# The first product of an MLP by seven products: the operands of the next block made by a table of 42 places

## The chip, the cores and the metric

The kernel runs on one core of one Trainium2 chip. The core has five engines with a queue of instructions each, taken strictly in order: TensorE (PE, with its weight loads as PEld), VectorE (DVE), ScalarE (ACT), GpSimd (POOL) and SyncE (SP), which here issues nearly all DMAs. An instruction that waits holds up everything behind it on its own engine. The metric is device time in microseconds (us) of one execution, lower is better.

## The reference

Two layers of self-attention and MLP run on a row matrix x of 2048 x 640 in float32, with a layer norm without weights ahead of each part:

```
x = x + attention(layernorm(x))         # 32 heads of 20
x = x + mlp(layernorm(x))               # 640 -> 1536 -> 640
mlp(y) = relu(y @ w1 + b1)**2 @ w2 + b2
(both lines twice, with the same weights)
```

What is changed here lies around `layernorm(x)` and `y @ w1`.

## The kernel before

Every layer has these stages: attention; the **heads** stage, which multiplies the attention's output by `wo` and adds x (`add_heads`); the **up** stage, the first product of the MLP (class `Up`); and the **down** stage, the second (class `Down`).

**Heads.** The 2048 rows are handled as 16 tiles of 128 rows, four tiles to a block, four blocks. A tile takes two chains of 15 matmuls, one per half of the 640 columns, each into a PSUM bank of its own; the banks are used in a ring of eight. After a chain DVE adds the old x (L1407), then a call of `side()` takes one step of side work, and after two chains SP stores the new row tile to `d_x`.

**Up.** Each block of 512 rows is multiplied by w1 with Strassen's scheme in Winograd's form: seven products of half-size matrices in place of eight. On the side of w1 the seven operands (A11, S2, S1, A22, S3, A12, S4) are made once and stored; on the side of the rows the operands are B11, T2, T1, T4, T3, B21, B22 for the first 512 of the 640 columns, and a plain part and a difference (`xd`) for the last 128. They are sums of four row tiles of the block: tiles 0 and 1 make one half, 2 and 3 the other, and the sums are formed of the pairs (0, 2) and (1, 3). Every float32 operand is split in two parts, a rounded one (`hi`, a copy by ACT, L375) and the rest (`lo`, a subtraction by DVE, L376, or by POOL, L342, for T3 and T4). A product is three matmuls per 128 columns: hi by hi, hi by lo, lo by hi.

A **unit** of the up stage is one of six column groups of w1: chains of 6 (A11), 9 (S4, of the unit before), 6 (S2), 6 (S1), 9 (A22), 9 (S3) and 9 (A12) matmuls, 54 in all, into four banks; the next unit uses the other four. S3 adds into the bank of S2, A12 into that of A11 and S4 into that of S1. DVE's own work in a unit, in its order: L1488 (after the S4 chain), L1465 (after S2; the S3 chain waits for it), then L1473, L1474 and L1475 after S3 (the next S4 chain waits for L1474). ACT does copies, bias with relu, and squares (L1454, L1460, L1477, L1490), POOL two sums at the unit's end (L1493, L342), SP the store of the result (`d_h`).

Between the chains of a unit `side()` is called seven times, 42 times in a block; each call runs one step that makes the operands of the **next** block. A **place** is the number of such a call in its block: place 7k + s is call s of unit k. Calls 2, 3 and 4 lie, for DVE, between L1465 and L1473; calls 5 and 6, and 0 of the next unit, between L1475 and L1488; call 1 between L1488 and L1465.

To make the operands of a block, each of its four row tiles is loaded (`x<-d_x`), its mean and variance taken (`stats`: L315 and L316 on DVE, L318 and L319 on POOL), normalised and turned in blocks of 32 (`turn`: L348 and L353 on DVE), stored to `d_t`, and read back across partitions by four DMAs (`turn_load`: `y<-d_t`). Then come the sums on POOL (L342) and the splits on ACT, DVE and POOL.

Before, all that is one generator, `forms`, whose `yield`s set the places. It takes about 31 of the 42 places of a block, from place 0 on: loads at place 0, `stats` of two tiles at 3 and 4, the first sums and the first split one line after the other in one place, and the split of T2 in the next. For block 0 the generator is run in the last two of the four blocks of the heads stage, three steps per call, and what is left is run at once at the end.

The arena of 42 slots holds the pieces of w1 (24 slots), the operands of two blocks and the results; SP allows eight DMAs to be under way.

Of the kernel before, what the change touches and what calls it, by code (L numbers as in the profile page):

```python
# [16 lines left out]
P = 128  # L17
# [5 lines left out]
KD = D // P  # L23
# [18 lines left out]
def tile_layers(  # L42
# [320 lines left out]
    def forms(qb, x_src, res, late):  # L363

        xs, ys, mvs = {}, {}, {}

        def view(y):
            return y.rearrange("p (a k i) -> p k a i", a=4, k=KD)

        def split(dst, src, i, lo):  # L370
# [4 lines left out]
            nc.scalar.copy(hi_, src)  # L375
            lo(lo_, src, hi_.bitcast(F32))  # L376

        def pair(i):
            a, b = view(ys[i]), view(ys.pop(i + 2))
            t = xtile("t").rearrange("p (k a i) -> p k a i", a=4, k=KD)  # L380
            k1, k2, k3 = slice(0, 2), slice(2, 4), slice(4, 5)
            if not res:
                for n in range(LAST + 2):
                    if n == LAST + 1:
                        res[n] = xpool.tile([P, 2, 1, 2 * P], F32R, tag="x", name=name("xd"))
                    elif n != B21 or not late:
                        res[n] = slot([P, 2, 2, 2 * P], F32R, "xf")
            dve = nc.vector.tensor_sub
# [7 lines left out]
            split(res[T1_], t[:, k1], i, dve)  # L396
            yield
            pool_lo(t[:, k3], a[:, k3], b[:, k3])
            pool_lo(t[:, k2], a[:, k2], t[:, k2])
            split(res[B22], b[:, k2], i, dve)  # L400
            yield
            split(res[T4_], t[:, k2], i, pool_lo)
            yield
            split(res[T3_], b[:, k1], i, pool_lo)
            yield
            for r, y in enumerate((a, b)):
                split(res[LAST][:, :, r : r + 1], y[:, k3], i, dve)
            split(res[LAST + 1], t[:, k3], i, dve)
            yield
            if not late:  # L410
                split(res[B21], a[:, k2], i, dve)
                del ys[i]
                yield

        def rest():
            res[B21] = slot([P, 2, 2, 2 * P], F32R, "xf")
            for i in range(2):
                split(res[B21], view(ys.pop(i))[:, 2:4], i, nc.vector.tensor_sub)

        def load(i):  # L420
            xs[i] = row_tile(x_src, qb * 4 + i)

        def turned(i):
            ys[i] = turn(xs[i], mvs.pop(i), i)
            del xs[i]

        load(0)
        load(2)
        yield
        yield  # L430
        yield
        for i in (0, 2):
            mvs[i] = stats(xs[i])
            yield
        load(1)
        load(3)
        yield
        for i in (0, 2):
            turned(i)
            yield  # L440
            yield
        for i in (1, 3):
            mvs[i] = stats(xs[i])
            yield
        turn_load(ys[0], 0)
        turned(1)
        yield
        turn_load(ys[2], 2)
        yield
        turned(3)  # L450
        yield
        yield
        yield
        turn_load(ys[1], 1)
        for n, _ in enumerate(pair(0)):
            if n == 1:
                turn_load(ys[3], 3)
            yield
        yield from pair(1)
        if late:  # L460
            late.append(rest)
# [1239 lines left out]
    def layer(first, x_a, x_m, x_e, front_0, ahead):  # L1701
# [26 lines left out]
        coming = first_forms = None  # L1728
# [10 lines left out]
        for _ in first_forms:  # L1739
            pass  # L1740
# [11 lines left out]
        firsts = list(range(16, w_1.n))  # L1752
        up = Up(side)
        for qb in range(NQB):
            nxt, late = {}, []
            if qb + 1 < NQB:
                late.append(None)
                coming_rows = forms(qb + 1, x_m, nxt, late)
                for n in range(7 * NP - 1):
                    steps.append(lambda n=n, f=coming_rows: (  # L1760
                        n % 2 == 1 and firsts and w_1.load(firsts.pop(0)), next(f, None)
                    ))
# [104 lines left out]
```

## Time and profile before

| what | before |
|---|---|
| median of 3 runs | 3612.69 us (3606.93 to 3617.94) |
| the profiled execution, and its span | 3612.81 us, 3610.7 us |
| busy PE, DVE, ACT, POOL | 97%, 77%, 79%, 27% of the span |
| matmuls of the up stage (L1427), idle ahead of them | 74.4 us |
| heads stage of the two layers, about | 1373 to 1444 us, 3172 to 3243 us |
| up stage of the two layers, about | 1444 to 1651 us, 3243 to 3453 us |
| mean granted clock of PE | 0.988 |

The profile is one execution on the chip. Matmuls are pipelined and overlap, so the busy share of PE says little of how much it does; idle time just before a group of instructions, and what ended it, says more. In rows of a timeline the columns are the start, the length, engine, line, operation, names and shapes, a count where rows were merged, and in square brackets the idle time of that engine just before and the instruction that ended it. Rows "SPq" are DMAs being issued.

### The profile page before, as it was taken

The numbers are of one execution on the slowest core, as the hardware profiler recorded it, in microseconds if no ns is written. First come the engines' busy times: TensorE is split into PE (matmuls) and PEld (weight loads), VectorE is DVE, ScalarE is ACT, GpSimd is POOL, SyncE is SP. The second block draws the span as 40 slices with busy tenths as digits, with TensorE's granted clock in tenths as the row PEclk, the third lists the DMA queues.
The fourth block names the chain that finished last, engine by engine and source line by source line (L and its number), as shares of the span: only waits on it lengthen the run. The fifth ranks groups of instructions, "written<-read, shape, count | busy, mean of one in ns | idle before, by whom it ended". The sixth has DMA issues, their size and how long they took to land. (4 is left out here: it accounts for less than half of the span.)

```text
span 3610.7 us, 74267 instructions
## 1 busy us (share of the span) xinstructions
PE 3519.4 (97%) x26404; PEld 2177.0 (60%) x26404; DVE 2771.0 (77%) x5512; ACT 2834.9 (79%) x5026; POOL 965.2 (27%) x1189
## 2 busy tenths in 40 slices
PE   9999999999999999789999999999999999997999
PEld 8997333333333338789989973333333333387899
DVE  8998888888888863556869988888888888545567
ACT  5889999999999992354348899999999999913533
POOL 4430444444412211340153202211221122113400
PEclk9999999999999999899999999999999999998999
DMA  7665444444322147648667652222232211476484
GB/s 258 223 217 179 133 146 145 123 136 126 119 61 57 48 125 258 233 159 299 230 195 231 194 165 66 69 81 60 63 83 56 56 50 51 131 267 221 170 288 147
DMA packets 335041, 534.46 MB, mean 148 GB/s; under 512 B 75604, under 2 KB 154964, under 8 KB 334672
## 3 DMA queue, kind: packets, MB, share of 16 engines
q1 hardware_dynamic: 334144, 528.02, 45.9%
q8 instruction: 209, 3.42, 0.4%
q10 hardware_dynamic: 528, 1.70, 0.2%
q14 instruction: 160, 1.31, 0.1%
HBM read 339.01 MB, written 190.55 MB: 147 GB/s over the span
## 5 line engine op out<-in xcount | busy, mean ns | idle before, releaser
L905 ACT ACTIVATE e<-banks 128x512 f32<-128x512 f32 (+1 forms) x3416 | 2035.2, 691 | 56.7 <-PE banks L895 20.3
L812 DVE TENSOR_REDUCE mx<-banks 128x1 f32<-128x512 f32 x2560 | 1620.5, 685 | 321.9 <-PE banks L801 269.2
L910 PE MATMUL banks<-e,vg 128*32 128x512 f32 x8192 | 1093.5, 605 | 2.1 <-ACT e L905 2.0
L801 PE MATMUL banks<-k,q 60*128 60x512 f32 x3360 | 1060.3, 410 | 0.0
L895 PE MATMUL banks<-q,k 62*128 62x512 f32 x4096 | 1049.7, 441 | 1.6 <-DMA d_v<-v 0.3
L895 PEld LDWEIGHTS banks<-q,k 62*128 62x128 f32 x4096 | 514.9, 184 | 749.5 <-ACT e L905 441.3
L801 PEld LDWEIGHTS banks<-k,q 60*128 60x128 f32 x3360 | 567.8, 185 | 195.1 <-ACT e L905 63.9
L841 DVE CUSTOM_DVE_ANT_0 rl<-banks,rl 128x512 f32<-128x512 f32 x736 | 477.0, 689 | 31.3 <-PE banks L801 7.0
L834 ACT ACTIVATE rl<-banks 128x512 f32<-128x512 f32 x736 | 399.6, 602 | 57.4 <-PE banks L801 45.7
L1427 PE MATMUL banks<-xf,w 128*128 128x256 f32 x2448 | 331.6, 297 | 74.4 <-DVE r L1474 64.9
L910 PEld LDWEIGHTS banks<-e,vg 128*32 128x32 f32 x8192 | 162.2, 108 | 352.9 <-issue 269.9
L1427 PEld LDWEIGHTS banks<-xf,w 128*128 128x128 f32 x2448 | 320.7, 205 | 81.9 <-DVE r L1474 68.6
L508 PE MATMUL banks<-xnT,wqk 64*128 64x512 f32 x1080 | 326.6, 392 | 0.0
L496 PE MATMUL banks<-xnT,wqk 64*128 64x512 f32 x1080 | 325.6, 393 | 0.0
L954 POOL TENSOR_TENSOR few<-few,minus_t 128x16 f32<-128x16 f32 x62 | 179.9, 2902 | 236.1 <-DMA few<-d_s 236.0
L339 POOL CAST mr<-nt 128x32 fp32r<-128x32 f32 x64 | 13.6, 212 | 751.1 <-DVE nt L867 751.1
L965 POOL TENSOR_TENSOR o<-o 128x512 f32<-128x512 f32 x62 | 79.6, 1284 | 500.1 <-DMA o<-d_r 276.6
L801 PE MATMUL banks<-kd,q 60*128 60x512 f32 x736 | 210.8, 398 | 1.1 <-ACT rl L834 0.5
L496 PEld LDWEIGHTS banks<-xnT,wqk 64*128 64x128 f32 x1080 | 199.2, 186 | 11.5 <-issue 1.7
L508 PEld LDWEIGHTS banks<-xnT,wqk 64*128 64x128 f32 x1080 | 201.2, 187 | 7.0
L496 PE MATMUL banks<-wv,xnT 64*128 64x320 f32 x960 | 193.5, 308 | 0.0
L1454 ACT ACTIVATE r<-r,b_t 128x512 f32<-128x512 f32 x96 | 59.2, 616 | 170.9 <-DVE r L1475 149.2
(149 smaller groups left out, 3656.4 us busy)
## 6 DMA issues: line engine op xcount, KB each, us to landing
q<-d_qk SPq DMA_DIRECT2D x876, 80.0 KB
d_qk<-ev SPq DMA_DIRECT2D x80, 512.0 KB
k<-d_qk SPq DMA_DIRECT2D x444, 80.0 KB
x<-d_x SPq DMA_DIRECT2D x96, 320.0 KB
w<-d_w SPq DMA_DIRECT2D x60, 480.0 KB
w<-d_w SPq DMA_DIRECT2D x48, 512.0 KB
d_h<-r SPq DMA_DIRECT2D x48, 512.0 KB
r<-d_h SPq DMA_DIRECT2D x48, 512.0 KB
```

The lines of the kernel that those rows point to most:

```text
L496: top = nc.tensor.matmul(dst, a[:64], b[:64], start=start, stop=last)
L508: low = nc.tensor.matmul(dst, a, b, start=False, stop=last, skip_group_check=True)
L801: nc.tensor.matmul(dst, q_t[t][b : b + 60, p, sub * P : (sub + 1) * P], k_t[t // NQB, c][b : b + 60, p, :], start=True, stop=True,)
L812: nc.vector.tensor_reduce(maxima(t)[:, 2 * p + par, sub, c : c + 1], dst, axis=AX.X, op=ALU.max)
L834: nc.scalar.activation(r, dst, AF.Relu)
L841: nc.vector.tensor_tensor_reduce(out=r[par], in0=dst, in1=r[par], scale=1.0, scalar=LEAST, op0=ALU.add, op1=ALU.max, accum_out=maxima(t)[: ...
L895: nc.tensor.matmul(dst, k_t[t // NQB, kt // 4][b : b + 62, p, (kt % 4) * P : (kt % 4 + 1) * P], q_t[t][b : b + 62, p, :], start=True, stop ...
L905: nc.scalar.activation(dst, src, AF.Exp, scale=SCALE)
L910: nc.tensor.matmul(acc[32 * h : 32 * h + 32, :], v_t[t // NQB, kt // 8][:, kt % 8, 32 * h : 32 * h + 32], es[p][:, par, :], start=(kt == 0 ...
L954: nc.gpsimd.tensor_tensor(few, few, minus_t, op=ALU.pow)
L965: nc.gpsimd.tensor_mul(o[:, 0, :], o[:, 0, :], o[:, 1, :])
L1427: nc.tensor.matmul(dst, w, v, start=n == 0 and not more, stop=n == len(todo) - 1, skip_group_check=more,)
```

## The change

The generator becomes a class `Forms` with one method for each step, and two tables say at which place which step stands. `PLACES` holds for the making of a block during the up stage of the block before: it uses the 42 places of that block and, by numbers below zero, the last nine places of the block before that (-9 is place 33, -4 place 38, -3 place 39). `BESIDE_HEADS` holds for block 0, by the number of the call in the heads stage (0 to 31); the steps -9, -4 and -3 of block 1 stand at calls 29, 30 and 31 there.

Loads, `stats`, `turned`, `fetch` (the four `y<-d_t` DMAs), sums and splits are now separate entries. The T1 and T2 splits stand three and four places behind their sums for the pair (0, 2) and three and five for (1, 3); T4's and T3's order is changed. The slots of the operands are taken when each is first written.

Also moved: the 24 pieces of w1 (`w_1.load`, 512 KB each) are loaded one at a time, 18 of them at calls 2 to 22 of the heads stage, two at 25 and 27, and the last four at places 1, 4, 7 and 10 of block 0 (before: four after each heads block, 16, and eight at odd places of block 0). In the last block the first reads of the down stage (`lead`) stand at places 27, 29 and 33 instead of 35, 36 and 39, and the rows at 31 instead of 37. No arithmetic is changed: each engine has as many instructions as before. The lines are shifted: L1407 is now L1441, L1465 L1499, L1473 to L1475 L1507 to L1509, L1488 L1522, L375 and L376 L458 and L459.

The core of the diff:

```diff
-    def forms(qb, x_src, res, late):
...
-            pool_lo(t[:, k1], b[:, k1], a[:, k1])
-            pool_lo(t[:, k2], b[:, k2], t[:, k1])
-            split(res[B11], a[:, k1], i, dve)
-            yield
-            pool_lo(b[:, k1], b[:, k2], b[:, k1])
-            split(res[T2_], t[:, k2], i, dve)
-            yield
...
+    class Forms:
+        PLACES = {
+            -9: [("load", 0), ("load", 2)],
+            -4: [("stats", 0)],
...
+            23: [("sums", 0), ("split", B11, 0)],
...
+            27: [("split", T2_, 0)],
...
+        BESIDE_HEADS = {
+            10: [("load", 0), ("load", 2)],
+            12: [("stats", 0)],
...
+        def do(self, places, n):
+            for what, *args in places.get(n, ()):
+                getattr(self, what)(*args)
...
-        for qb in range(NQB):
-            if qb == 2:
-                first_forms = forms(0, x_m, x := {}, [])
-            if qb > 1:
-                steps.extend([lambda: [next(first_forms, None) for _ in range(3)]] * 7)
-            add_heads(qb, x_a, x_m, xs, side)
-            for s in range(qb * 4, qb * 4 + 4):
-                w_1.load(s)
...
+        weights_at = {g: 1 for g in [*range(2, 8), *range(9, 15), *range(17, 23), 25, 27]}
...
+        def between():
+            side()
+            n = beside[0]
+            made[0].do(Forms.BESIDE_HEADS, n)
+            made[1].do(Forms.PLACES, {29: -9, 30: -4, 31: -3}.get(n))
+            more(weights_at.get(n, 0))
+            beside[0] += 1
...
-                todo = {35: down.fetch, 37: lambda: down.rows(0), 36: down.fetch, 38: down.make,
-                        39: down.fetch, 41: down.make}
...
+        lead = {27: down.fetch, 29: down.fetch, 31: lambda: down.rows(0), 33: down.fetch,
+                38: down.make, 41: down.make}
...
+                    if qb + 1 < NQB:
+                        made[qb + 1].do(Forms.PLACES, n)
+                        if qb + 2 < NQB:
+                            made[qb + 2].do(Forms.PLACES, n - 7 * NP)
+                        if n % 3 == 1:
+                            more(1)
```

How the instructions stand, at three places. **SP, from the heads stage into block 0.** The rows of block 1 are `x_16670` and `x_16672` before, `x_16636` and `x_16638` now; a `d_x` target is the store of a finished row tile of the heads stage, `w` a piece of w1. Before:

```order
L78 DMA d_x_112<-x_16302 128x640
L78 DMA d_x_112<-x_16359 128x640
L78 DMA d_x_112<-x_16428 128x640
L78 DMA w_16654<-d_w_99 128x1024
L78 DMA w_16656<-d_w_99 128x1024
L78 DMA w_16658<-d_w_99 128x1024
L78 DMA w_16660<-d_w_99 128x1024
L78 DMA x_16670<-d_x_112 128x640
L78 DMA x_16672<-d_x_112 128x640
```

Now, and behind it what DVE has there:

```order
L78 DMA d_x_112<-x_16331 128x640
L78 DMA x_16636<-d_x_112 128x640
L78 DMA x_16638<-d_x_112 128x640
L78 DMA d_x_112<-x_16385 128x640
L78 DMA d_x_112<-x_16431 128x640
L78 DMA x_16696<-d_x_112 128x640
L78 DMA x_16698<-d_x_112 128x640
L78 DMA w_16700<-d_w_99 128x1024
```

```order
L1441 TENSOR_TENSOR x_16431<-banks,x_16431 128x320
L315 BN_STATS bst_16657<-x_16636 128x6 x2
L316 BN_AGGR mv_16658<-bst_16657 128x2
L1441 TENSOR_TENSOR x_16431<-banks,x_16431 128x320
L315 BN_STATS bst_16680<-x_16638 128x6 x2
L316 BN_AGGR mv_16681<-bst_16680 128x2
L1499 TENSOR_TENSOR us_16688<-banks,us_16688 128x256
L348 TENSOR_SCALAR y_16709<-x_16636,mv_16658 128x5x4x32
```

The first two rows of block 1 are loaded ahead of the last two stores and no longer behind four pieces of w1, and DVE takes their statistics ahead of and behind the last addition of the heads stage; before, they stood behind L1465 of the first unit.

**DVE, block 1, where the first sums and splits of block 2 stand.** `xf` are operands, `t` tiles that POOL's sums write, `y` turned rows. Before (unit 2):

```order
L1465 TENSOR_TENSOR us_17415<-banks,us_17415 128x256
L376 TENSOR_TENSOR xf_17459<-y_17310,xf_17459 128x2x128
L376 TENSOR_TENSOR xf_17460<-t_17458,xf_17460 128x2x128
L1473 TENSOR_TENSOR us_17415<-banks,us_17415 128x256
L1474 TENSOR_TENSOR r_17496<-banks,us_17415 128x2x128
```

Now (units 3 and 4):

```order
L1499 TENSOR_TENSOR us_17490<-banks,us_17490 128x256
L459 TENSOR_TENSOR xf_17526<-y_17268,xf_17526 128x2x128
L459 TENSOR_TENSOR xf_17537<-y_17347,xf_17537 128x2x128
L459 TENSOR_TENSOR xf_17549<-y_17268,xf_17549 128x128
L459 TENSOR_TENSOR xf_17549<-y_17347,xf_17549 128x128
L1507 TENSOR_TENSOR us_17490<-banks,us_17490 128x256
L1508 TENSOR_TENSOR r_17563<-banks,us_17490 128x2x128
L1509 TENSOR_TENSOR r_17563<-banks,us_17490 128x2x128
L459 TENSOR_TENSOR xf_17569<-t_17523,xf_17569 128x2x128
L459 TENSOR_TENSOR xf_17588<-t_17523,xf_17588 128x2x128
```

A split that reads a sum (`t`) no longer stands ahead of the unit's L1473; the splits there read rows that came with a DMA.

**DVE, block 1, unit 5 and the start of block 2.** Before:

```order
L1465 TENSOR_TENSOR us_17696<-banks,us_17696 128x256
L1473 TENSOR_TENSOR us_17696<-banks,us_17696 128x256
L1474 TENSOR_TENSOR r_17749<-banks,us_17696 128x2x128
L1475 TENSOR_TENSOR r_17749<-banks,us_17696 128x2x128
L376 TENSOR_TENSOR xf_17767<-y_17310,xf_17767 128x2x128
L376 TENSOR_TENSOR xf_17767<-y_17395,xf_17767 128x2x128
```

Now:

```order
L1499 TENSOR_TENSOR us_17689<-banks,us_17689 128x256
L459 TENSOR_TENSOR xf_17588<-t_17645,xf_17588 128x2x128
L315 BN_STATS bst_17731<-x_17669 128x6 x2
L316 BN_AGGR mv_17732<-bst_17731 128x2
L315 BN_STATS bst_17747<-x_17671 128x6 x2
L316 BN_AGGR mv_17748<-bst_17747 128x2
L1507 TENSOR_TENSOR us_17689<-banks,us_17689 128x256
L1508 TENSOR_TENSOR r_17763<-banks,us_17689 128x2x128
L1509 TENSOR_TENSOR r_17763<-banks,us_17689 128x2x128
L459 TENSOR_TENSOR xd_17642<-t_17645,xd_17642 128x128
L459 TENSOR_TENSOR xf_17785<-y_17268,xf_17785 128x2x128
L459 TENSOR_TENSOR xf_17785<-y_17440,xf_17785 128x2x128
```

In unit 5, where DVE had no side work ahead of L1473, a split of T2 and the statistics of two rows of the block after next now stand there.

More of the change, by code (lines that the diff above doesn't have):

```diff
@@ L415, in rest @@
-        def rest():
-            res[B21] = slot([P, 2, 2, 2 * P], F32R, "xf")
-            for i in range(2):
[L418 to L458, printed above, removed]
@@ L459, in forms, with split @@
-        yield from pair(1)
-        if late:
-            late.append(rest)
+        def split(self, n, i):
+            if n not in self.res:
+                self.res[n] = slot([P, 2, 2, 2 * P], F32R, "xf")
+            src = {
+                B11: lambda: self.view(i)[:, 0:2],
+                B21: lambda: self.view(i)[:, 2:4],
+                B22: lambda: self.view(i + 2)[:, 2:4],
+                T1_: lambda: self.t[i][:, 0:2],
+                T2_: lambda: self.t[i][:, 2:4],
+                T4_: lambda: self.t[i][:, 2:4],
+                T3_: lambda: self.view(i + 2)[:, 0:2],
+            }[n]()
+            self.into(self.res[n], src, i, pool_lo if n in (T3_, T4_) else nc.vector.tensor_sub)
+            if n == T3_:
+                del self.y[i + 2]
@@ new lines, in plain, with diff, late @@
+        def plain(self, i):
+            if LAST not in self.res:
+                self.res[LAST] = slot([P, 2, 2, 2 * P], F32R, "xf")
+            for r in range(2):
+                self.into(self.res[LAST][:, :, r : r + 1], self.view(i + 2 * r)[:, 4:5], i)
+        def diff(self, i):
+            if LAST + 1 not in self.res:
+                self.res[LAST + 1] = xpool.tile([P, 2, 1, 2 * P], F32R, tag="x", name=name("xd"))
+            self.into(self.res[LAST + 1], self.t.pop(i)[:, 4:5], i)
+        def late(self):
+            for i in range(2):
+                self.split(B21, i)
+                del self.y[i]
@@ L1772, in layer @@
             all_steps()
-            if late:
-                for _ in coming_rows:
-                    pass
+            made[qb].res = None
+            if qb + 1 < NQB:
                 del x[B21]
-                late[1]()
-            x = nxt
+                made[qb + 1].late()
+        del x
         up.flush()
```

136 lines of the change are left out of this document (86 added, 50 removed).

## The prediction

> **What bounds the kernel now.** I read the page first, then what PE waits for, then PE's timeline through the two up stages, then the queues of DVE, ACT and SP where PE stands still.
>
> ```profile
> span 3610.7 us, 74267 instructions
> L1427 PE MATMUL banks<-xf,w 128*128 128x256 f32 x2448 | 331.6, 297 | 74.4 <-DVE r L1474 64.9
> ```
>
> Of PE's little idle time 74.4 us stand ahead of L1427, the change's stage, and 64.9 of them end with DVE's L1474. But PE also runs slowly after a pause, so idle time is not the whole loss. The matmuls with `xd` come once in each unit and mark it. PE's timeline, layer 1, then layer 2:
>
> ```profile
> 1444.01 0.87 PE L1427 MATMUL banks<-xf,w 128*128 128x256 f32 x6
> 1450.98 0.51 PE L1427 MATMUL banks<-xd,w 128*128 128x256 f32 x3
> 1463.29 5.12 PE L1427 MATMUL banks<-xf,w 128*128 128x256 f32 x27 [8.52 <-DVE r L1474]
> 1486.42 5.45 PE L1427 MATMUL banks<-xf,w 128*128 128x256 f32 x27 [7.99 <-DVE r L1474]
> 1497.08 5.00 PE L1427 MATMUL banks<-xf,w 128*128 128x256 f32 x27 [1.98 <-DVE r L1474]
> 1514.87 0.52 PE L1427 MATMUL banks<-xd,w 128*128 128x256 f32 x3
> 1515.23 6.28 PE L1427 MATMUL banks<-xf,w 128*128 128x256 f32 x51
> 1547.00 3.50 PE L1427 MATMUL banks<-xf,w 128*128 128x256 f32 x27 [1.42 <-DVE r L1474]
> 1564.23 0.52 PE L1427 MATMUL banks<-xd,w 128*128 128x256 f32 x3
> 1613.96 0.52 PE L1427 MATMUL banks<-xd,w 128*128 128x256 f32 x3
> 1620.44 0.52 PE L1427 MATMUL banks<-xd,w 128*128 128x256 f32 x3
> 1651.04 1.04 PE L1582 MATMUL banks<-w,hb 128*128 128x320 f32 x6
> ...
> 3242.80 2.11 PE L1427 MATMUL banks<-xf,w 128*128 128x256 f32 x13
> 3246.92 0.90 PE L1427 MATMUL banks<-xd,w 128*128 128x256 f32 x3
> 3313.58 0.52 PE L1427 MATMUL banks<-xd,w 128*128 128x256 f32 x3
> 3363.30 0.52 PE L1427 MATMUL banks<-xd,w 128*128 128x256 f32 x3
> 3413.15 0.52 PE L1427 MATMUL banks<-xd,w 128*128 128x256 f32 x3
> 3453.39 1.80 PE L1582 MATMUL banks<-w,hb 128*128 128x320 f32 x6
> ```
>
> An undisturbed unit takes 1620.44 - 1613.96 = 6.48 us, 0.12 for each of its 54 matmuls; a block of six 38.88. So the loss of each stretch is: to the first `xd` 6.97 less 24 x 0.12 = 4.1; block 0 to 1 63.89 - 38.88 = 25.0; 1 to 2 49.36, so 10.5; 2 to 3 49.73, so 10.9; the rest 37.08 less five units and 30 matmuls (36.0) 1.1. Layer 1 loses **51.6**. Layer 2 likewise: 4.12, so 1.2; 66.66, so 27.8; 49.72, so 10.8; 49.85, so 11.0; 40.24, so 4.2: **55.0**. Together **106.6 us** is all that this change can take away. Of it 74.4 are idle time; most of the other 32 are slow matmuls behind pauses: 27 of them took 5.00 to 5.45 us rather than 3.24.
>
> What DVE stood at while PE waited (rows of DVE and ACT):
>
> ```profile
> 1460.37 0.89 DVE L315 BATCH_NORM_STATS2 bst<-x 128x6 f32<-128x320 f32 x2 [8.79 <-DMA x<-d_x]
> 1534.98 0.49 DVE L376 TENSOR_TENSOR xf<-t,xf 128x256 fp32r<-128x256 f32 x1 [3.57 <-ACT xf L375]
> 1534.55 0.41 ACT L375 CAST xf<-t 128x256 fp32r<-128x256 f32 x1 [3.93 <-POOL t L342]
> 1532.98 0.72 POOL L342 TENSOR_TENSOR t<-y,y 128x256 f32<-128x256 f32 x1 [0.97 <-DMA y<-d_t]
> ```
>
> DVE is not short of time, it is blocked at the head of its queue: once for rows still on their way, else for a T2 split whose ACT copy waits for POOL's sum, which waits for the read-back. L1473 and L1474 stand behind it.
>
> **The change, part by part.** No instruction is added, so what counts is where each one waits.
>
> *The two kinds of stall removed.* Loads now stand five places or more (5 x 6.48 / 7 = 4.6 us) ahead of their statistics, the read-back eight and six places (7.4, 5.6 us) ahead of the sums, T2 four and five (3.7, 4.6 us) behind them; POOL's two sums take about 1.5 us. Today the sum of 1532.98, with no place between it and the read-back, waited 0.97. So the pauses of 8.52 and 7.99 and DVE's 3.57 of a steady block have lost their cause. That takes all of the 106.6 away but what follows.
>
> *What is late next: unit 5.* I walked the new order with lengths and pitches of these rows (ACT, then DVE):
>
> ```profile
> 1547.31 0.72 ACT L1454 ACTIVATE r<-r,b_t 128x512 f32<-128x512 f32 x1 [1.69 <-DVE r L1475]
> 1548.06 0.63 ACT L1477 ACTIVATE r<-r 128x512 f32<-128x512 f32 x1
> 1548.60 0.39 ACT L375 CAST xf<-t 128x256 fp32r<-128x256 f32 x1
> 1548.89 0.47 ACT L1454 ACTIVATE r<-banks,b_t 128x256 f32<-128x256 f32 x1
> 1549.56 0.37 ACT L1460 COPY us<-banks 128x256 f32<-128x256 f32 x1
> 1510.84 0.41 DVE L1475 TENSOR_TENSOR r<-banks,us 128x256 f32<-128x256 f32 x1
> 1514.71 0.88 DVE L315 BATCH_NORM_STATS2 bst<-x 128x6 f32<-128x320 f32 x2
> 1516.74 0.37 DVE L1473 TENSOR_TENSOR us<-banks,us 128x256 f32<-128x256 f32 x1
> ```
>
> Undisturbed, the S3 chain (1515.23) begins 4.0 us after L1475's end (1511.25), and needs L1465 (now L1499). In unit 5 ACT has relu 0.75, square 0.54, B22 0.29, relu 0.37, two plain copies of half the size at an estimated 0.2 each, L1460's copy 0.26 and T1 0.41 between: 3.0; then DVE's T1 split, L1488 and L1465 at about 0.37 each, the length of L1473: 4.1. With `diff` and B11 at place 32, which push L1475 of unit 4 back by 0.5, S3 waits about 0.8. Next T2 (its copy stands behind ACT's relu and square of the tail, about 1.5 after L1488) and two statistics of 2.03 us (1514.71 to 1516.74) stand ahead of L1473: L1474 ends 4.4 after L1465, while PE needs it 24 matmuls, 2.9 us, after S3's start: 1.5 more. Unit 0 of the next block has T4, `diff` and two B21 in the same stretch and starts late: 0.8. Sum 3.1, and about 0.9 for the clock (1.42 idle cost 3.50 - 3.24 = 0.3, 1.98 cost 1.8): **4.0** for block 0 to 1 and 1 to 2. Block 2 to 3 has no statistics behind T2: 0.8 + 0.3, **1.0**. Bounds: 0, if ACT keeps pace, and 10.7 each, what a steady block loses today.
>
> The Trainium skill, "TensorE: Matmul & The Clock Gate" (What's actually happening), has the clock halved only after an idle window of about 3.4 us. By that rule gaps like these cost no clock, and the time would be about 4 us lower. The trace does not agree: 27 matmuls behind 1.98 us of idle took 5.00.
>
> *The heads stage.* The window of it in layer 1 and one where DMA was full (the last two columns are the share of the DMA engines and GB/s), the weights issued in that stage, two groups of DVE, and rows of DVE and SP:
>
> ```profile
> 1372.00:1444.00 72.00, 72.00 (x490) 70.87 (x483) 32.13 (x59) 3.98 (x12) 8.69 (x16) 1.00 0.81 278
> 1660.00:1680.00 20.00, 17.78 (x110) 17.25 (x109) 12.70 (x27) 6.78 (x14) 0.00 (x0) 0.91 1.02 385
> w<-d_w SPq DMA_DIRECT2D x12, 512.0 KB
> 1413.41 0.49 DVE L1407 TENSOR_TENSOR x<-banks,x 128x320 f32<-128x320 f32 x1 [1.71 <-PE banks L476]
> L348 DVE TENSOR_SCALAR y<-x,mv 128x640 f32<-128x640 f32 x8 | 7.4, 919 | 0.0
> L353 DVE STREAM_TRANSPOSE x<-y 128x640 f32<-128x640 f32 x8 | 6.8, 846 | 0.3
> 1420.32 0.89 DVE L315 BATCH_NORM_STATS2 bst<-x 128x6 f32<-128x320 f32 x2 [6.42 <-DMA x<-d_x]
> 1412.44 2.69 SPq L78 DMA_DIRECT2D x<-d_x  x4
> ```
>
> DVE has 1.71 us free per chain; the dearest added step, one tile normalised and turned, is 0.92 + 0.85 = 1.77. DVE gets late (by some 5 us where rows are late, as at 1420.32) and catches up; PE has eight banks, 7 x 2.2 = 15 us, before it notices. **0** for PE. DMA: 72 us at 278 GB/s are 20.0 MB, with 12 pieces of w1 issued; now 20 pieces and two more rows, 4.9 MB more: 346 GB/s. The stage's own ratio (278 at 0.81) makes 343 at full share, the other window shows 385. So it just fits, or the last loads come up to 7 us late, if the four pieces issued at the old stage's end are counted too (27 MB / 343 = 79).
>
> The Trainium skill, "DMA: Bandwidth & Descriptors" (Where 436 GB/s comes from), limits one core to about 358 GB/s at the HBM. By it 27 MB take 75 us, 3 more than the stage has; the trace disagrees with 385 over 20 us.
>
> *Start of block 0.* The load of block 1's rows waits on SP for the store of tile 13 and on POOL's last T4 split for its buffer: I put it at 1442, and its landing 4.5 us later (four rows issued from 1412.44 were there at 1420.3, 7.9; two in less). DVE, with the last addition and L1465 behind it, then needs 1.03 + 0.45 + 1.0 + 0.41: L1465 ends at about 1449.4, and S3 could start at 1444.0 + 2.9 = 1446.9. Wait 2.5, clock 2: **4.5** a layer, where 4.1 and 1.2 are lost today; between 0 and 12 (the 7 us above). Behind it the pause of 8.52 is gone: the queue holds one piece of w1 where it held eight and four stores.
>
> *End.* `lead` reads the down stage's first operands eight places earlier; **0.5** left of 1.1 and 4.2. Down itself is unchanged.
>
> Sum for a layer: 4.5 + 4.0 + 4.0 + 1.0 + 0.5 = 14; two layers 28. Gain 106.6 - 28 = 78.6. The profiled execution took 3612.8 us (span 3610.7), 0.1 above the median of the runs: 3612.8 - 78.6 = **3534 us**.
>
> **Rivals.**
>
> *Only the long pauses go.* DVE and ACT do the same work, and each of the three makings loses 10.7 as a steady block does today: (4.5 + 32.1 + 0.5) x 2 = 74; 3580 us. For it: DVE's heavy places are now spread over six units instead of four, so more units are near their limit. Against: the dearest pause in those 10.7 hangs on the T2 split behind its sum (DVE's 3.57 at 1534.98, and the slow clock behind it), which is undone.
>
> *Nearly all goes.* Unit 5 keeps pace, loads land in time: start 2, end 0.5, 1 per block: 11 in all, 3517 us.
>
> *Every block becomes like block 0: slower.* SP is in order, and loads and read-backs are now set behind stores of a unit's result that wait for its last squares. If rows reach DVE as late as at 1460.37 in each making, with the read-back late too, each block loses 26 as block 0 does: (4.5 + 78 + 0.5) x 2 = 166, 59 more than now: 3672 us. It is slower than today as soon as the three lose over 16 each. Against: in a steady block the loads have no weights ahead of them, and today's land in time there.
>
> *It doesn't do what it says.* If L1474 is late because DVE and ACT are full and not because they are blocked, moving steps changes nothing: 3613. Against: DVE's 8.79 and 3.57 us of idle while PE waits for it.
>
> **How the numbers follow.** Forecast 0.74, own range 3520 to 3552; only the long pauses 0.10; nearly all 0.09; slower 0.03; no change 0.04. For 8 in 10 the range takes in the third case and the dearer unit 5 and start: 3512 to 3564. A measurement tells about 0.3%, 11 us. Faster: 0.74 + 0.10 + 0.09 = 0.93; same 0.04; slower 0.03.
>
> **What would show it.** PE's idle time ahead of the up stage's matmuls falls from 74 us to about 20 in two layers; no DVE row there waits over 3 us for `x<-d_x` or for a split's copy, but for one at the heads stage's end; the distance of first to last `xd` of a block is about 43 us, 43 and 40; the longest waits left end with L1508 at the seam of unit 5 and the next block. The heads stage shows PE without a pause at about 350 GB/s. I am wrong if statistics at the heads stage's end wait over 8 us, if PE pauses within the heads stage, or if units 3 and 4 still show waits over 1 us.

## The result, and the profile after

The change takes **3550.4 us** (median of four runs, 3548.1 to 3552.2) where the kernel before takes 3612.4: a ratio of 0.983 (95% interval 0.981 to 0.985), 62 us less. The forecast was 3534 (3512 to 3564), 78.6 us less. The profiled execution took 3550.9 us, its span 3548.8.

The page has this of the span and of the up stage's matmuls; L1461 is L1427 of before:

```profile
span 3548.8 us, 74211 instructions
L1461 PE MATMUL banks<-xf,w 128*128 128x256 f32 x2448 | 315.3, 288 | 26.7 <-DVE r L1508 10.4
```

The idle time ahead of them fell from 74.4 to 26.7 us, their busy time from 331.6 to 315.3: the pauses and the slow matmuls behind them went together, 64 us. PE's timeline after, layer 1, in the rows that answer to those of before (layer 2 has the same rows at its seams, and 0.65, 1.66 and 1.39 us of waiting at its start):

```profile
1444.55 0.87 PE L1461 MATMUL banks<-xf,w 128*128 128x256 f32 x6
1448.48 0.39 PE L1461 MATMUL banks<-xf,w 128*128 128x256 f32 x1 [3.06 <-ACT xf L458]
1450.53 3.99 PE L1461 MATMUL banks<-xf,w 128*128 128x256 f32 x17 [1.66 <-DVE xf L459]
1454.32 0.84 PE L1461 MATMUL banks<-xd,w 128*128 128x256 f32 x3
1456.15 8.10 PE L1461 MATMUL banks<-xf,w 128*128 128x256 f32 x51 [0.99 <-DVE us L1499]
1464.09 0.52 PE L1461 MATMUL banks<-xd,w 128*128 128x256 f32 x3
...
1488.07 3.49 PE L1461 MATMUL banks<-xf,w 128*128 128x256 f32 x27 [0.60 <-DVE r L1508]
1492.73 3.13 PE L1461 MATMUL banks<-xf,w 128*128 128x256 f32 x24 [0.81 <-DVE us L1499]
1497.48 3.72 PE L1461 MATMUL banks<-xf,w 128*128 128x256 f32 x27 [1.62 <-DVE r L1508]
1501.04 0.52 PE L1461 MATMUL banks<-xd,w 128*128 128x256 f32 x3
1501.85 6.38 PE L1461 MATMUL banks<-xf,w 128*128 128x256 f32 x51 [0.29 <-DVE us L1499]
...
1545.03 0.52 PE L1461 MATMUL banks<-xd,w 128*128 128x256 f32 x3
1587.03 0.52 PE L1461 MATMUL banks<-xd,w 128*128 128x256 f32 x3
1623.74 1.04 PE L1616 MATMUL banks<-w,hb 128*128 128x320 f32 x6
```

The pauses of 8.52 and 7.99 us are gone. What is left sits in two places. At the **start**, PE waits 3.06 and 1.66 us for operands of block 0 itself, and the first full unit runs at a slow clock (51 matmuls take 8.10 us where 6.28 is usual, at a mean granted clock of 0.76). At each **seam** of two blocks stand the four short waits of 0.60, 0.81, 1.62 and 0.29.

The loss of each stretch, worked out from such rows as in the prediction (the time from one `xd` to the next less what undisturbed matmuls take), in us, layer 1 / layer 2. "To block 1" also holds what the start spills into the first unit. The rows below the second are the experiments:

| kernel | start | to block 1 | to 2 | to 3 | end | both layers | median |
|---|---|---|---|---|---|---|---|
| before | 4.1 / 1.2 | 25.0 / 27.8 | 10.5 / 10.8 | 10.9 / 11.0 | 1.1 / 4.2 | 106.6 | 3612 |
| the change | 6.9 / 4.2 | 7.8 / 6.3 | 5.1 / 5.1 | 3.1 / 3.1 | 0.7 / 1.2 | 43.6 | 3550.4 |
| `late_loads_w` | 1.7 / 4.3 | 15.9 / 14.2 | 3.2 / 3.1 | 3.1 / 4.0 | 0.7 / 1.2 | 51.4 | 3556.1 |
| `late_loads` | 6.0 / 5.3 | 7.0 / 5.7 | 3.1 / 3.1 | 3.1 / 4.2 | 0.7 / 1.2 | 39.4 | 3546.1 |
| `t2` | 8.8 / 3.3 | 7.4 / 9.6 | 7.6 / 7.6 | 5.8 / 5.8 | 0.4 / 0.8 | 57.0 | 3562.4 |
| `lead` | 7.6 / 6.5 | 6.1 / 6.1 | 5.1 / 5.1 | 3.1 / 3.1 | 2.1 / 4.5 | 49.2 | 3556.3 |
| `nx12` | 6.0 / 1.7 | 7.8 / 9.0 | 5.1 / 5.1 | 3.1 / 3.1 | 0.9 / 1.2 | 43.0 | 3547.8 |
| `thin` | 0 / 0 | 9.5 / 8.0 | 5.1 / 5.1 | 3.1 / 3.1 | 0.7 / 1.2 | 35.8 | 3541.6 |
| `mid` | 0 / 0 | 8.3 / 5.1 | 5.1 / 5.1 | 3.1 / 3.1 | 0.7 / 1.2 | 31.7 | 3538.4 |
| `seam` | 7.7 / 6.8 | 4.8 / 4.2 | 5.8 / 4.6 | 2.8 / 3.3 | 0.7 / 1.2 | 41.7 | 3549.0 |
| `seam12` | 4.9 / 3.6 | 2.9 / 3.2 | 3.3 / 3.3 | 3.3 / 3.3 | 1.0 / 1.2 | 30.0 | 3536.8 |
| `best1` | 0 / 0 | 4.1 / 5.5 | 3.3 / 2.8 | 3.3 / 3.3 | 0.7 / 1.2 | 24.1 | 3529.4 |
| `best2` | 0 / 0 | 3.5 / 4.6 | 4.0 / 4.0 | 4.0 / 4.0 | 0.7 / 1.2 | 26.0 | 3531.4 |

A difference of a few us between medians is not to be told from none; the stretches tell more. The steady seams come out alike to 0.1 us from one kernel to the next where nothing was changed in them (5.1 and 3.1), the start does not (6.9 and 7.6, 4.2 and 6.5 with the same order), so a start counts only where it moves by more than 3 us.

### The profile page after: what moved, and what is told of

Same layout as the page of the kernel before. It is cut to its first block, busy times and chain, and to the rows that moved or that the text cites. A ratio compares the mean times of both kernels' runs of the same rounds, so it can differ in the third digit from the quotient of the medians.

```text
span 3548.8 us, 74211 instructions
## 1 busy us (share of the span) xinstructions
PE 3503.0 (99%) x26404; PEld 2161.2 (61%) x26404; DVE 2776.4 (78%) x5512; ACT 2833.4 (80%) x5026; POOL 965.2 (27%) x1189
## 5 line engine op out<-in xcount | busy, mean ns | idle before, releaser
L1461 PE MATMUL banks<-xf,w 128*128 128x256 f32 x2448 | 315.3, 288 | 26.7 <-DVE r L1508 10.4
L1461 PEld LDWEIGHTS banks<-xf,w 128*128 128x128 f32 x2448 | 303.1, 194 | 36.0 <-DVE r L1508 14.2
L530 PE MATMUL banks<-wv,xnT 64*128 64x320 f32 x960 | 193.5, 308 | 0.0
L542 PE MATMUL banks<-wv,xnT 64*128 64x320 f32 x960 | 190.4, 306 | 0.0
```

What stands on the lines that cost most here:

```text
L530: top = nc.tensor.matmul(dst, a[:64], b[:64], start=start, stop=last)
L542: low = nc.tensor.matmul(dst, a, b, start=False, stop=last, skip_group_check=True)
L1461: nc.tensor.matmul(dst, w, v, start=n == 0 and not more, stop=n == len(todo) - 1, skip_group_check=more,)
```

## The experiments

Three questions were open: which part of the change took the long pauses away, why the start of block 0 lost more than forecast, and what the seams cost.

**Which part removed the pauses.** `late_loads_w` undoes the early loads and the spread of the weights; `late_loads` undoes the early loads alone.

```diff
-            -9: [("load", 0), ("load", 2)],
-            -4: [("stats", 0)],
-            -3: [("stats", 2)],
-            0: [("load", 1), ("load", 3)],
-            2: [("turned", 0)],
+            0: [("load", 0), ("load", 2)],
+            3: [("stats", 0)],
+            4: [("stats", 2)],
+            5: [("load", 1), ("load", 3)],
+            6: [("turned", 0)],
# fetch 0 goes from 8 to 12; late_loads_w also has:
-        weights_at = {g: 1 for g in [*range(2, 8), *range(9, 15), *range(17, 23), 25, 27]}
+        weights_at = {g: 4 for g in (7, 15, 23, 31)}
-                        if n % 3 == 1:
+                        if n % 2 == 1:
```

> The rows of the next block are loaded again at places 0 and 5 and their statistics taken at 3, 4, 10 and 12 (as before the change), and the pieces of w1 are loaded again by fours, at calls 7, 15, 23 and 31 of the heads stage, and at the odd places of block 0. The making of block 0 and all the splits stay as in the change. Theory 'rows behind the weights': the loads of block 1 stand behind pieces of w1 on SP again, DVE waits 5 to 9 us for x ahead of L1507 in unit 0 of block 0, PE pauses near 8 us there, and block 0 to 1 loses 16 to 22 us in place of 7.8 and 6.3: about 3565 us. Blocks 1 to 3 have no weights in the queue and lose no more than 5 each. Theory 'the splits alone made the pauses': with the splits spaced no pause comes back in block 0: 3545 to 3552 us.

> As the last one, but with the pieces of w1 as in the change (20 in the heads stage, four at places 1 to 10). Theory 'rows behind the weights': only one piece and the last stores stand ahead of the loads, DVE waits 2 to 5 us for x in unit 0 of block 0; block 0 to 1 loses 9 to 13 us: about 3554 us. Theory 'three places are too few at any time': the blocks 1 and 2 also show waits for x<-d_x of over 1 us, and lose 3 us or more above the 5.1 and 3.1 of the change: 3565 us.

`late_loads_w` took 3556.1 us, `late_loads` 3546.1 (0.982 of before, 0.980 to 0.983; not to be told from the change). Layer 1 of `late_loads_w`, PE, DVE and SP:

```profile
1461.20 5.20 PE L1460 MATMUL banks<-xf,w 128*128 128x256 f32 x27 [9.05 <-DVE r L1507]
1458.28 0.89 DVE L315 BATCH_NORM_STATS2 bst<-x 128x6 f32<-128x320 f32 x2 [9.32 <-DMA x<-d_x]
1446.54 2.30 SPq L78 DMA_DIRECT2D w<-d_w  x4
1450.28 1.28 SPq L78 DMA_DIRECT2D x<-d_x  x2
```

and of `late_loads`:

```profile
1458.85 4.98 PE L1460 MATMUL banks<-xf,w 128*128 128x256 f32 x27 [2.73 <-DVE r L1507]
1455.93 0.89 DVE L315 BATCH_NORM_STATS2 bst<-x 128x6 f32<-128x320 f32 x2 [3.25 <-DMA x<-d_x]
```

With four pieces of w1 and a store just ahead of the rows on SP the long pause is back, 9.05 us where it was 8.52, and 6.73 in layer 2. With the weights spread it is 2.73, and 1.94 in layer 2. So with rows loaded late, **where the weights stand** decides over most of that pause, and the early loads take the rest. How much the early loads would do alone is not shown: no run has them with the weights by fours, where they would stand ahead of the last four pieces too. In blocks 1 and 2 the statistics at places 3 and 4 wait for their rows once in two layers, 0.88 us, and the seam to block 2 costs 3.1 us where the change has 5.1. Statistics set early, in unit 5, cost 2 us at that seam, and the same at the seam to block 1, and bring nothing there. Neither theory had counted this, so both kernels came out 8 to 9 us faster than the theory about the weights, which fits their rows, had said.

`t2` puts the split of T2 one place behind its sums again:

```diff
-            24: [("third", 0), ("split", B22, 0)],
+            24: [("split", T2_, 0), ("third", 0), ("split", B22, 0)],
-            27: [("split", T2_, 0)],
-            33: [("third", 1), ("split", B22, 1)],
+            33: [("split", T2_, 1), ("third", 1), ("split", B22, 1)],
-            37: [("split", T2_, 1), ("fourth", 1)],
+            37: [("fourth", 1)],
```

> The split of T2 stands one place behind its sums again (24 and 33 in place of 27 and 37), all else as in the change. Theory 'the split behind its sum blocks DVE': ACT's copy waits for POOL's second sum, DVE behind it, L1507 and L1508 come late in units 3 and 4: each making of a block loses 1.5 to 6 us more, six makings 9 to 36 us: about 3570 us. Theory 'it was the late read-back': with the read-backs where they are now the sums are done in time and the split costs nothing there: 3549 to 3552 us.

It took 3562.4 us, 12 more. Block 1, PE, DVE, ACT and POOL:

```profile
1574.65 5.00 PE L1460 MATMUL banks<-xf,w 128*128 128x256 f32 x27 [2.83 <-DVE r L1507]
1571.78 0.50 DVE L458 TENSOR_TENSOR xf<-t,xf 128x256 fp32r<-128x256 f32 x1 [2.58 <-ACT xf L457]
1571.34 0.41 ACT L457 CAST xf<-t 128x256 fp32r<-128x256 f32 x1 [2.94 <-POOL t L342]
1568.18 0.74 POOL L1526 TENSOR_TENSOR us<-r 128x256 f32<-128x256 f32 x1 [4.89 <-ACT r L1523]
```

The read-back is in time here, and DVE still waits 2.58 us for ACT's copy, which waits for POOL's sum: POOL has its two sums of the unit's tail first (1568.18). PE then stands 2.83 us, and 27 matmuls behind it take 5.00. The steady seams go from 5.1 and 3.1 to 7.6 and 5.8, 2.6 each: the spacing of T2 is a cause of its own, at the lower end of what was expected.

`lead` puts the down stage's first reads back to places 35, 36, 37 and 39.

> The change with the first reads of the down stage at their old places 35, 36, 37 and 39. What the earlier reads brought: theory 'they took 3 us from the end of the up stage in layer 2': its end loses 4 us again in place of 1.15, the down stage's first wait is about 1.5 in place of 5.2 us, and the whole differs by less than 2 us from the change. Rival 'the wait of 5.2 us in the down stage is of another make': it stays above 4 and the whole is 3 us slower than the change, about 3553 us.

3556.3 us. The end of layer 2, its last chain and the first wait of the down stage:

```profile
3392.61 1.56 PE L1461 MATMUL banks<-xf,w 128*128 128x256 f32 x9 [3.46 <-DVE r L1508]
3410.27 0.65 PE L1616 MATMUL banks<-w,hb 128*128 128x320 f32 x2 [4.23 <-ACT hb L327]
```

The end loses 4.5 again in place of 1.2, so the earlier reads are worth 3.3 us in layer 2 and 1.3 in layer 1; that is 4.6 of the 6 us by which this kernel is slower. The down stage's wait for a read of `d_h`, 1.36 us before and 5.23 in the change, stays at 4.23, as the rival had it: the earlier reads made at most 1 us of it. What made the rest is open; no run took it apart.

**The start of block 0.** Rows of the change's heads stage that had not been forecast, DVE, ACT and SP:

```profile
1419.12 0.89 DVE L315 BATCH_NORM_STATS2 bst<-x 128x6 f32<-128x320 f32 x2 [4.69 <-DMA x<-d_x]
1430.90 0.94 DVE L348 TENSOR_SCALAR y<-x,mv 128x640 f32<-128x640 f32 x1 [6.79 <-DMA d_t<-x]
1443.41 0.41 ACT L458 CAST xf<-y 128x256 fp32r<-128x256 f32 x1 [4.51 <-DMA y<-d_t]
1435.47 2.56 SPq L78 DMA_DIRECT2D y<-d_t  x4
1439.30 3.17 SPq L78 DMA_DIRECT2D y<-d_t  x4
```

and two slices of 8 us (the last two columns are the share of the DMA engines and GB/s):

```profile
1392.00:1400.00 8.00, 8.00 (x57) 8.00 (x56) 1.92 (x4) 0.00 (x0) 0.00 (x0) 1.00 1.02 391
1416.00:1424.00 8.00, 8.00 (x56) 8.00 (x55) 4.77 (x11) 0.10 (x1) 1.47 (x4) 1.00 1.04 345
```

From 1392 to 1432 us the DMA engines are full. DVE waits for rows, and at 1430.90 for a buffer: the new `y` takes that of a row tile whose store to `d_t` has not landed. The read-backs of tiles 1 and 3 are issued at 1435 and 1439 and come after the up stage has begun. Is it the buffer, or the weights ahead in the queue? `nx12` has a 12th buffer (`NX = 12`), `thin` 12 pieces of w1 in the heads stage in place of 20, `mid` 15, the last three behind the read-backs:

```diff
-        weights_at = {g: 1 for g in [*range(2, 8), *range(9, 15), *range(17, 23), 25, 27]}
+        weights_at = {g: 1 for g in [*range(2, 8), *range(9, 15)]}               # thin
+        weights_at = {g: 1 for g in [*range(2, 8), *range(9, 15), 24, 27, 30]}   # mid
-                        if n % 3 == 1:
+                        if n % 2 == 1:                                           # thin
```

> One more buffer in the pool of row tiles (12 in place of 11), nothing else. Theory 'buffer': the tile that DVE waited 6.79 us for (y of row tile 3 takes the buffer of a row tile whose store to d_t had not landed) is free in time; row tile 3 is turned some 5 us sooner, its read-back too, and the loss at the start of the up stage (6.9 + 3.3 us in layer 1, 4.2 + 1.8 in layer 2) falls by about 4 to 5 per layer: some 3541 us. Theory 'full DMA': the transfers then only queue elsewhere, the read-back lands as late as now: 3549 to 3551 us, and the start loses as much. In both the seams between blocks (about 4.6, 5.1 and 3.1 us) stay as they are.

> 12 pieces of w1 in the heads stage in place of 20, the other 12 at the odd places 1 to 23 of block 0. That takes 4.2 MB, about 12 us at the measured 343 GB/s, out of the heads stage. Theory 'full DMA': rows and read-backs of block 0 land sooner, the start of the up stage loses 2 to 4 us a layer instead of 10.2 and 6.0: about 3540 us. Theory 'buffer': DVE's wait for the buffer of a row tile stays near 6.8 us and so does the loss: 3547 to 3551 us. If the weights now come too late for the units of block 0, that shows as waits of PE for w: 3555 us and more.

> 15 pieces of w1 in the heads stage (six at calls 2 to 7, six at 9 to 14, and at 24, 27 and 30, behind the read-backs) and nine at the places 1, 4, 7 ... 25 of block 0. Theory 'full DMA' (the run with 12 pieces lost nothing at the start, but read-backs of block 1 came late behind weights in block 0, 9.5 and 8.0 us): start loses under 1 us, block 0 to 1 about 5 as the others do: 14 and 14.5 a layer, about 3534 us. Rival: three pieces late in the heads stage, or the fifth one more in block 0, are enough to make it late at one end: as with 12 pieces, 3540 us or more.

The buffer alone: 3547.8 us, not to be told from the change. DVE's 6.79 falls to 1.37, but the last read-back is issued only 1.9 us sooner:

```profile
1426.06 0.94 DVE L348 TENSOR_SCALAR y<-x,mv 128x640 f32<-128x640 f32 x1 [1.37 <-DMA d_x<-x]
1437.38 3.38 SPq L78 DMA_DIRECT2D y<-d_t  x4
```

Fewer weights: 3541.6 and 3538.4 us, and the start loses nothing in either layer. In `thin` PE runs from the heads stage into a whole unit without a wait, but meets longer ones in block 0, where ACT waits for a read-back behind the weights moved there:

```profile
1444.18 3.04 PE L1461 MATMUL banks<-xf,w 128*128 128x256 f32 x24
...
1471.70 3.49 PE L1461 MATMUL banks<-xf,w 128*128 128x256 f32 x27 [1.80 <-DVE r L1508]
1480.70 4.94 PE L1461 MATMUL banks<-xf,w 128*128 128x256 f32 x27 [2.02 <-DVE r L1508]
1478.99 0.40 ACT L458 CAST xf<-y 128x256 fp32r<-128x256 f32 x1 [1.83 <-DMA y<-d_t]
```

In `mid` both read-backs are issued one behind the other from 1431.08 on, 4.4 and some 6 us before the change's, and DVE's wait for the buffer is 2.77 us without a 12th one. The start is thus set by **the weights ahead of block 0's rows**, and most of the wait for the buffer follows from them: the store that frees it stands behind weights too. `mid` did not reach its 3534: in layer 1 it still loses 8.3 us to block 1, with a wait of 2.79 us in unit 5, where a read-back stands behind two weights.

**The seams.** `seam` takes the statistics out of unit 5 and `xd` of the first pair out of the stretch ahead of L1507:

```diff
-            -4: [("stats", 0)],
-            -3: [("stats", 2)],
-            2: [("turned", 0)],
+            2: [("stats", 0)],
+            3: [("stats", 2)],
+            6: [("turned", 0)],
-            28: [("fourth", 0)],
+            28: [("diff", 0), ("fourth", 0)],
-            32: [("diff", 0), ("sums", 1), ("split", B11, 1)],
+            32: [("sums", 1), ("split", B11, 1)],
# fetch 0 from 8 to 12; the tile t is freed behind the later of T4 and xd; seam12 also has NX = 12
```

> The statistics of the first two rows of a block go from places 38 and 39 of the block before to places 2 and 3 of unit 0, with turned 0 at 6 and its read-back at 12 behind them, and the difference xd of the first pair goes from place 32 to 28. Theory 'order': the waits of 1.62 (statistics ahead of L1507 in unit 5) and 0.60 (xd behind ACT's copies ahead of L1507 in unit 4) go, those of 0.81 and 0.29 stay. A seam loses about 2.2 us in place of 4.6, 5.1 and 3.1: 6 us a layer, about 3538 us. Theory 'full engines': DVE and ACT have no room there, the wait goes to unit 0 or 1, where the statistics stand now: 3548 to 3552 us.

> The run with the statistics at places 2 and 3 and xd at 28, and one more buffer in the pool of row tiles. There ACT's copy L1494 of unit 5 stood idle 1.13 us before it wrote a new us tile and S3 then waited 1.89 for L1499. Theory 'buffer': with 12 buffers that idle time is gone, S3 waits about 0.8 again, a seam loses about 2.5 us (in place of 3.8, 5.8 or 4.6, and 2.8 or 3.3), 7 to 9 us less in two layers: about 3539 us. Theory 'ACT and DVE are full there': 3546 to 3549 us, the 1.89 stays.

`seam` took 3549.0 us: nothing gained. Of the waits with L1508 (here L1515) the 1.62 went, as in the theory. The 0.60 only fell to 0.45, and S3 of unit 4 got a wait of 0.32: moving `xd` brought nothing. And S3 of unit 5 waited 1.89 us in place of 0.81, for L1499 of the change, which is L1506 here. PE at two seams of it, and ACT ahead of the first:

```profile
1493.31 6.50 PE L1468 MATMUL banks<-xf,w 128*128 128x256 f32 x51 [1.89 <-DVE us L1506]
1536.57 7.87 PE L1468 MATMUL banks<-xf,w 128*128 128x256 f32 x51 [1.89 <-DVE us L1506]
1491.45 0.37 ACT L1501 COPY us<-banks 128x256 f32<-128x256 f32 x1 [1.13 <-PE banks L1468]
```

The profile puts ACT's 1.13 us down to PE, but that chain had long ended: the copy is the first to write a new `us` tile. With one more buffer, in `seam12`, the same rows read:

```profile
1486.83 6.48 PE L1468 MATMUL banks<-xf,w 128*128 128x256 f32 x51 [0.81 <-DVE us L1506]
1484.82 0.37 ACT L1501 COPY us<-banks 128x256 f32<-128x256 f32 x1
```

3536.8 us, 12 less than without the buffer and 14 less than the change. Half of the 12 is a shorter start, which no run explains; the seams and ends alone lose 27.4 us in the change, 25.9 in `seam` and 20.9 in `seam12`. So the rival "full engines" falls and the order is confirmed for the statistics, not for `xd`, with a second cause behind it: in the new order the next tile waited for a buffer of the pool. `late_loads` gets there without a 12th buffer: it has the statistics at places 3 and 4, but loads their rows only at place 0, and its seams and ends alone lose 20.5 us.

**Together.** `best1` is `mid`, `seam` and the 12th buffer; `best2` moves copies out of the stretch from L1509 to L1499 as well:

```diff
-            27: [("split", T2_, 0)],
-            28: [("diff", 0), ("fourth", 0)],
-            30: [("split", T3_, 0)],
-            31: [("split", T4_, 0)],
-            32: [("sums", 1), ("split", B11, 1)],
+            28: [("diff", 0), ("split", T3_, 0)],
+            30: [("split", T2_, 0), ("fourth", 0)],
+            31: [("split", B11, 1)],
+            32: [("split", T4_, 0), ("sums", 1)],
-            35: [("split", T1_, 1)],
-            37: [("split", T2_, 1), ("fourth", 1)],
+            37: [("split", T1_, 1), ("split", T2_, 1), ("fourth", 1)],
```

> The three that helped together: 15 pieces of w1 in the heads stage, 12 buffers for row tiles, statistics at places 2 and 3 and xd at 28. Theory 'separate places' (the weights cost at the start, the order and the buffer at the seams): start 0 to 0.5 as with 15 pieces alone, seams about 3 each as in the run with 12 buffers, end 1: 10 to 11 a layer, 21 in all where 43.6 are lost now, about 3528 us. Rival 'they share a cause': the later weights in block 0 hold up read-backs, block 0 to 1 loses 5 to 8 again: 3533 to 3537 us.

> As the last, and copies moved out of the stretch of ACT and DVE between L1509 and L1499 of units 4 and 5: T2 of the first pair at 30, T3 at 28, B11 of the second pair at 31, T4 of the first at 32, T1 of the second at 37. Theory 'ACT's and DVE's chain from L1509 to L1499 sets S3': the waits of 0.32 (unit 4) and 0.8 (unit 5) fall to 0 to 0.3, and a seam loses 1.5 us in place of 3.2: 8 to 10 us less than the last in two layers if L1508 stays in time, about 3519 us. Rival 'the load only moves': L1507 and L1508 of the same units come later by what was moved, 0.4 to 0.8 us: no more than 3 us less.

`best1`: **3529.4 us**, 0.977 of before (0.976 to 0.979), 21 less than the change. Its 21 us are most of the 12 and 14 of `mid` and `seam12`, so the causes are nearly separate ones; the largest rest is the 5.5 us "to block 1" of layer 2, where a read-back still stands behind two weights. `best2` took 3531.4: the rival was right. PE at its steady seam:

```profile
1520.18 3.49 PE L1466 MATMUL banks<-xf,w 128*128 128x256 f32 x27 [0.50 <-DVE r L1513]
1524.92 3.14 PE L1466 MATMUL banks<-xf,w 128*128 128x256 f32 x24 [0.89 <-DVE us L1504]
1528.57 3.73 PE L1466 MATMUL banks<-xf,w 128*128 128x256 f32 x27 [0.51 <-DVE r L1513]
```

Against `best1` the wait of 0.33 in unit 4 went; the one in unit 5 rose from 0.80 to 0.89, the one of 0.44 with L1508 (here L1513) to 0.50, and a new one of 0.51 with it came behind: what left one stretch arrived in the other, and a seam costs 4.0 us in place of 3.3.

## Why the prediction was right, and where not

Forecast: 106.6 us of loss, 28 of it left. Measured: 43.6 left. The 15.6 between them by the forecast's terms:

| term, both layers | forecast | measured | off by |
|---|---|---|---|
| start of block 0, with its spill into unit 1 | 9.0 | 6.9 + 3.3 + 4.2 + 1.8 = 16.2 | +7.2 |
| block 0 to 1, the seam alone | 8.0 | 4.55 x 2 = 9.1 | +1.1 |
| block 1 to 2 | 8.0 | 10.2 | +2.2 |
| block 2 to 3 | 2.0 | 6.2 | +4.2 |
| end | 1.0 | 1.9 | +0.9 |

**Right.** The views pointed at the right thing: PE's loss hung on DVE's queue being blocked, and unblocking it gave 63 of the 106.6 us. The walk through unit 5 gave 0.8 for S3 and 1.5 for L1474; the rows show 0.81 and 1.62. (The terms given for S3 add up to 0.6, 4.1 - 4.0 + 0.5, so that 0.8 met 0.81 so closely is luck.) PE did not pause within the heads stage, and DMA moved 341 GB/s there (346 forecast). "Only the long pauses go" is out: the steady seams did not keep their 10.7. So is "every block becomes like block 0": no block came near 26. The earlier reads of the down stage brought 3.4 us at the end against before, 4.6 against `lead`, where 4.3 were forecast.

**Wrong: the start.** The step that failed is "*Start of block 0*": it walked only the statistics of block 1's rows and took block 0's own operands to be ready. The longest waits left, 3.06 and 1.66 us, are for these operands, and stand at the start, not at the seams as the prediction's signs had it; PE's idle time came out at 26.7 us, not about 20. The sum of bytes was right, but "it just fits" over 72 us says nothing on which transfers are late: the weights stand ahead of the last rows, stores and read-backs of block 0, and `thin` and `mid` lose nothing there. In `best1` the heads stage of layer 1 is as full as in the change, 348 GB/s at a share of 0.97 (341 at 0.97), and its start loses nothing: a full stage alone does not make the start late. That the last loads could be up to 7 us late stood as a bound; it should have been the forecast.

**Mis-sized: the seams, in both directions.** The wait of 0.60 ahead of S4 in unit 5 was missing: the push of 0.5 by `diff` and B11 at place 32 was counted for S3, not for the chain that waits for L1474 itself. Unit 0 waited 0.29, not 0.8. For the clock 0.9 was forecast; it was granted in full at all seams of the change, and 0.25 to 0.5 us behind each wait took that place. That block 0 to 1 came so near is thus in part luck. The forecast for block 2 to 3, 1.0, had only S3's wait; the rows of that seam have 0.60, 0.80 and 0.29, some 0.25 us more for the matmuls behind each, and smaller losses of about 0.3 each in units 3 and 4.

**Right sum, wrong share.** The forecast laid the removed pause of 8.52 to the earlier loads and the shorter queue together. With late loads the queue did most of it (9.05 to 2.73 us); what the early loads would do with the old queue was not run. In the later blocks the early loads spared one wait of 0.88 us in two layers, and the early statistics cost 2 us at each of the seams to blocks 1 and 2.

**Wrong by a little: "Down itself is unchanged."** Its first wait in layer 2 grew from 1.36 to 5.23 us; the stages behind that up stage took 2.1 us longer. `lead` clears the earlier reads of most of it.

## What to carry to other kernels

When work is moved earlier, list for each transfer what stands ahead of it on its queue, stores and bulk weights too: that a stage's bytes fit its time does not say that the urgent ones come first. Set a use behind its producer by the length of the whole chain, the producer engine's other duties included, and count the buffers that the new order holds longer: one more buffer was worth nothing at the seams until the order was right, and 5 us then, while loading the rows later, as in `late_loads`, did as much without it. Once the blocked heads of queues are gone, moving single steps between stretches of a full unit may only move the wait, as in `best2`.

## What the runs showed of the hardware

**The clock.** How long PE may stand before its clock drops could be read closely. Behind 1.80 us, 27 matmuls took 3.49 us; behind 2.02 us, 4.94 (`thin`, above). Behind 1.89 us both happened in one kernel, the 6.50 and 7.87 of `seam`. And in `mid` a pause of 2.79 us cost no clock at all, 24 matmuls behind it taking 3.13 us:

```profile
1485.83 3.13 PE L1461 MATMUL banks<-xf,w 128*128 128x256 f32 x24 [2.79 <-DVE us L1499]
```

So the length of a pause alone does not decide. The granted clock changes only on a fixed grid: in each of the 13 kernels every change in its record stands a whole number of steps of 3.413 us behind the one before. Windows cut on this grid, two of `seam` around 1536.57, then two of `mid` around 1485.83 (the third column is PE's busy time; the last three are the granted clock, the DMA share and GB/s):

```profile
1533.18:1536.59 3.41, 1.52 (x14) 1.31 (x12) 2.34 (x6) 1.45 (x6) 0.90 (x2) 1.00 0.69 260
1536.59:1540.01 3.42, 3.42 (x16) 3.42 (x17) 1.84 (x4) 1.37 (x4) 2.46 (x4) 0.50 0.04 14
1481.09:1484.50 3.41, 1.96 (x17) 1.75 (x15) 2.23 (x4) 1.84 (x6) 2.38 (x4) 1.00 0.88 304
1484.50:1487.91 3.41, 2.08 (x17) 2.08 (x18) 2.21 (x6) 1.74 (x4) 1.43 (x3) 1.00 0.12 43
```

The pause of 1.89 us lies in one window, and the next one has half the clock. The pause of 2.79 us is split over two windows, 1.45 and 1.33 us, and costs none. From 1430 to 1660 and from 3195 to 3460 us of all 13 kernels the full clock went on behind 1750 windows, none with PE idle for more than 1.82 us, and halved behind 64, none with PE idle for less than 1.65. So a pause at full clock costs itself and 0.25 to 0.5 us; where about 1.7 us or more of PE's idle time falls into one window, the clock halves for at least one window, and 27 matmuls take 1.5 us longer still. The Trainium skill, "TensorE: Matmul & The Clock Gate" (What's actually happening), has the gate watch a free-running window of about 3.4 us, and close after an idle one. The traces agree on the window and its length; that half a window of idle is enough does not fit a window that must be idle throughout.

**DVE beside POOL.** A DVE subtraction of 128x256 took 0.41 us alone and 0.97 with POOL at work beside it all the time; of POOL's own two there, one kept its 0.73 and the other took 0.91 in place of 0.72 (`seam12`):

```profile
1480.35 0.97 DVE L458 TENSOR_TENSOR xf<-y,xf 128x256 fp32r<-128x256 f32 x1 [1.82 <-ACT xf L457]
1485.69 0.41 DVE L458 TENSOR_TENSOR xf<-t,xf 128x256 fp32r<-128x256 f32 x1
1480.30 0.73 POOL L342 TENSOR_TENSOR r<-r 128x256 f32<-128x256 f32 x1
1480.99 0.91 POOL L342 TENSOR_TENSOR xf<-y,xf 128x256 fp32r<-128x256 f32 x1
1481.87 0.72 POOL L342 TENSOR_TENSOR xf<-t,xf 128x256 fp32r<-128x256 f32 x1
```

In that kernel 38 such subtractions ran with POOL idle and took 0.40 to 0.43 us; 40 had POOL beside them for most of their time and took 0.56 to 0.97. The prediction had priced all of these at one length. The Trainium skill, "GPSIMD Engine Reference" (1. Specifications), says that POOL shares its way to the memory with VectorE where DVE reads two inputs from it; the rows agree.
